# Sparse attention into a top-1 mixture of experts: v by 64-token tiles with neighbours copied in SBUF, loads farther ahead, x turned a tile ahead, lists used a pair later

## Chip, cores, metric

One core of one Trainium2 chip. The metric is the device time of one execution in microseconds (us), on the slowest (here the only) core. Before: 350.13 us, median of 3 runs (349.48 to 355.3).

## The reference

Block-sparse attention over 4 batches of 768 tokens with 8 heads of 64, then a mixture of 8 experts in which each token goes to one expert.

```python
# attention: block 32, window 16; 24 summary rows per head
k_sum = k.reshape(B, H, nb, block, D).max(axis=3)
v_sum = v.reshape(B, H, nb, block, D).mean(axis=3)
mask_l = np.abs(pos[:, None] - pos[None, :]) < window
# softmax over [q k^T masked by the window, q k_sum^T + log(block)], times [v, v_sum]
# experts, on x = attention output, 3072 x 512
logits = x @ w_gate + modality_bias[modality_id]
e_idx = np.argmax(logits, axis=1)
h = np.maximum(x[mask] @ w1[e], 0.0)                  # for each expert e
out[mask] = gate_w[mask, None] * (h @ w2[e])
```

## The kernel before

Attention works by pairs of heads: 16 pairs, 4 to a batch. A 64-token tile needs its own 64 keys and values, 16 neighbours on each side, and 24 summary rows. `features` turns the finished x of a pair, `route` picks experts after a batch, scatters the token rows to `xs` in DRAM (sorted by expert) and makes a list of tiles of 256 tokens of one expert; `expert_tile` computes one such tile. `pump()` puts one step of a tile between the steps of the next pairs, so that TensorE has two jobs to choose from. The last five tiles have no attention left beside them: the tail.

v goes from the load to a copy with a column of ones, to a scratch in DRAM, and back as overlapping windows:

```python
def values_in(n):
    vr = vrs[n % NV]
    nc.gpsimd.tensor_copy(vr[:, :, :, 0:D]..., vns.pop(n))
    nc.sync.dma_start(vscr[n % NV][16:S + 16]..., vr...)
def values_windows(n):
    nc.sync.dma_start(vws[n % NV][0:WK]...,
        bass.AP(a.tensor, a.offset, [[w, WK], [64 * w, NT], [1, w]]))
# ... (cut)
def expert_tile(i):
    xr = prep.pop(i)
    for c in range(NCD):
        for s2 in range(2):
            nc.tensor.transpose(px[:, c, s2, :], xr[:, s2, ts(c, 128)], ident)
    yield
    nc.vector.tensor_copy(xg, px...)
    # first layer ph (4 steps), Relu to hT, second layer pmo (2 steps), scaled rows to out (cut)
# ... (cut) the loop over pairs n = (b, cc)
    load(n + 3); scores(n, 1); values(n, 0); ...; values(n, 1); pump(); features(n)
    # list of batch b - 1 drained at cc == 0, its tiles from cc == 1, route(b) at cc == NP - 1
```

Names in the lines below: PE is TensorE, PEld its weight loads, DVE VectorE, ACT ScalarE, POOL GpSimd, SP SyncE with its DMA queue SPq. kn and qn are keys and queries as loaded, kb the keys with their neighbours, vw (later vb) the same for v, vs the summary rows of v and pv the matmuls that make them. pss are the scores, pT the masked weights, po the weighted values, xb the finished x, pt its turned (transposed) form. Of a tile, xr is x as loaded from `xs`, px its turned form and xg the copy of that, ph and pmo the matmuls of the two layers, ot the scaled rows. A line "A <- B" of the waits says that A stood idle until B was done.

The softmax here doesn't subtract the row's maximum and nothing guards it: scores larger than these inputs give would overflow.

## Time and profile before

| | before |
|---|---|
| span of the profiled execution | 358.2 us |
| first tile's turning px starts | 107.6 us |
| counts of the last batch known (pc) | 278.1 us |
| from first px to pc | 170.5 us |
| from pc to the end | 80.1 us |

These three stages are a first stage in which the DMA engines are nearly full, a middle in which tiles and attention share TensorE (PE), and an end. The busy totals (busy us, share of the span, instructions) say that no engine is near the bound over the whole span:

```profile
PE 198.4 (55%) x2359; PEld 135.1 (38%) x2359; DVE 137.7 (38%) x424; ACT 92.0 (26%) x169; POOL 107.9 (30%) x155
```

The profiled execution was some 8 us longer than the timed ones, which the prediction scales by 0.977; where in the span the excess lies isn't known.

In the middle alone, the windows view for PE (stretch, its length, PE busy us, granted clock, DMA share, GB/s):

```profile
107.60:278.10 170.50, 118.59 (x1379) 0.79 0.36 86
```

So 170.5 - 118.6 = 51.9 us of the middle are holes of PE.

### The profile page before, as it was taken

The page shows a single profiled execution, that of the slowest core. Times are in us where ns is not written, and L with a number is a line of the kernel's source. Part 1 is how long each engine was busy: PE and PEld are TensorE (multiplying, and loading weights), DVE is VectorE, ACT ScalarE, POOL GpSimd, SP SyncE. Part 2 cuts the span into 40 slices and gives each one's busy share as a digit, 9 for nine tenths or more (in the row PEclk, how much of TensorE's full clock was granted, in tenths as well). Part 3 has the DMA queues.
Part 4 walks back from the last instruction along what each step waited for, and adds up shares of the span by engine and source line. Part 5 has one row for each costly group of instructions (what it writes and reads, how often), then busy time and mean ns, then how long its engine had stood idle before and what let it go on. Part 6 is the DMA issues. An engine that isn't in the chain of part 4 may idle for free. (4 is left out here: it accounts for less than half of the span.)

```text
span 358.2 us, 6200 instructions
## 1 busy us (share of the span) xinstructions
PE 198.4 (55%) x2359; PEld 135.1 (38%) x2359; DVE 137.7 (38%) x424; ACT 92.0 (26%) x169; POOL 107.9 (30%) x155
## 2 busy tenths in 40 slices
PE   1140517264516957552395773969759003988860
PEld 1030416153404644341264542545536002566630
DVE  4230825458522336572124455523452700222210
ACT  1250316232501423151142412423302000222220
POOL 3981307006820050646003254021122510122220
PEclk9999999999999988855589885869897655899995
DMA  5999989943990253279431715050010273041110
GB/s 70 148 161 210 210 171 169 186 124 77 186 210 5 66 117 76 109 135 191 101 77 77 132 60 159 25 161 33 29 61 15 103 249 105 23 127 61 59 36 2
DMA packets 51606, 38.64 MB, mean 108 GB/s; under 512 B 29808, under 2 KB 46704, under 8 KB 51568
## 3 DMA queue, kind: packets, MB, share of 16 engines
q0 software_dynamic: 16880, 23.11, 31.9%
q1 hardware_dynamic: 34688, 15.06, 17.9%
q8 instruction: 20, 0.33, 0.4%
q14 instruction: 18, 0.15, 0.1%
HBM read 90.06 MB, written 15.58 MB: 295 GB/s over the span
## 5 line engine op out<-in xcount | busy, mean ns | idle before, releaser
L470 PE MATMUL ph<-xg,w1b 128*128 128x256 f16 x416 | 66.0, 323 | 34.5 <-DVE xg L464 31.7
L483 POOL DMA_INDIRECT out_dram<-ot,xr x26 | 25.9, 996 | 134.7 <-DVE ot L482 125.2
L470 PEld LDWEIGHTS <-w1b 128*128 128x128 f16 x416 | 45.0, 113 | 48.0 <-issue 36.4
L477 PE MATMUL pmo<-w2b,hT 128*128 128x512 f16 x208 | 50.8, 395 | 0.3 <-ACT hT L473 0.3
L473 ACT ACTIVATE hT<-ph 128x512 f16<-128x512 f32 x52 | 30.5, 599 | 74.7 <-PE ph L470 74.7
L257 ACT ACTIVATE pT<-pss 128x384 f16<-128x384 f32 x64 | 27.9, 486 | 52.1 <-PE pss L253 46.8
L358 POOL DMA_INDIRECT xs<-xb,posi x24 | 24.3, 1014 | 54.4 <-DVE tot L363 19.8
L258 DVE TENSOR_TENSOR pT<-pT,bmask 96x768 f16<-96x768 f16 x32 | 19.2, 600 | 45.6 <-ACT pT L257 45.2
L482 DVE TENSOR_SCALAR ot<-pmo,xr 128x512 f32<-128x512 f32 x26 | 19.3, 744 | 40.2 <-PE pmo L477 39.7
L272 PE MATMUL po<-vw,pT 120*64 120x65 f16 x384 | 15.3, 228 | 27.5 <-DVE pT L258 14.1
L461 PE MATMUL px<-ident,xr 128*128 128x128 f16 x104 | 9.2, 240 | 37.0 <-DMA xr<-xs 37.0
L233 ACT COPY qT<-pq 128x768 f16<-128x768 f16 x16 | 12.8, 802 | 63.0 <-PE pq L231 44.0
L477 PEld LDWEIGHTS <-hT 128*128 128x128 f16 x208 | 19.9, 100 | 22.9 <-issue 2.4
L217 ACT COPY kb<-pk 128x1152 f16<-128x1152 f16 x16 | 17.9, 1119 | 35.7 <-PE pk L215 28.7
L288 PE MATMUL pt<-ident,xb 128*128 128x128 f16 x96 | 12.9, 274 | 20.7 <-DVE xb L279 20.4
L272 PEld LDWEIGHTS <-pT 120*64 120x64 f16 x384 | 11.5, 137 | 33.7 <-issue 18.3
L461 PEld LDWEIGHTS <-xr 128*128 128x128 f16 x104 | 7.2, 108 | 38.8 <-DMA xr<-xs 37.1
L222 DVE TENSOR_TENSOR km<-kb 128x384 f16<-128x384 f16 x16 | 6.8, 426 | 38.4 <-ACT kb L217 38.4
L253 PE MATMUL pss<-qT,kb 64*128 64x64 f16 x384 | 14.9, 220 | 11.8 <-DVE kb L226 7.7
L92 POOL COPY vr<-vn 96x1024 f16<-96x1024 f16 x16 | 17.7, 1108 | 8.0 <-DMA vn<-in_v_dram 7.9
L279 DVE TENSOR_TENSOR xb<-po,rec 128x384 f16<-128x384 f32 x32 | 17.8, 557 | 1.3
L288 PEld LDWEIGHTS <-xb 128*128 128x128 f16 x96 | 7.8, 117 | 24.5 <-DVE xb L279 23.1
(123 smaller groups left out, 226.7 us busy)
## 6 DMA issues: line engine op xcount, KB each, us to landing
w1b<-in_moe_w_dram POOLq DMA_DIRECT2D x15, 1024.0 KB
w2b<-in_moe_w_dram POOLq DMA_DIRECT2D x15, 1024.0 KB
vw<-vscr SPq DMA_DIRECT2D x16, 292.5 KB
xr<-xs SPq DMA_DIRECT2D x13, 258.0 KB
vscr<-vr SPq DMA_DIRECT2D x16, 195.0 KB
kn<-in_k_dram POOLq DMA_DIRECT2D x16, 192.0 KB
qn<-in_q_dram POOLq DMA_DIRECT2D x16, 192.0 KB
vn<-in_v_dram POOLq DMA_DIRECT2D x16, 192.0 KB
```

Source lines behind the costliest of these rows:

```text
L217: nc.scalar.copy(kb[:, :, 0:WK].rearrange("p t (s c) -> p t s c", c=C8), bass.AP(pk.tensor, pk.offset, [pk.ap[0], [8, NT], [1, WK // C8], ...
L257: nc.scalar.activation(pT[:, h], pss[h], AF.Exp, scale=SCALE)
L258: nc.vector.tensor_tensor(pT[0:WK], pT[0:WK], bmask[0:WK, None, 6 * half:6 * half + 6, :].to_broadcast([WK, 2, 6, 64]), op=ALU.mult)
L272: nc.tensor.matmul(po[64 * (tl % 2):64 * (tl % 2) + 64, h, tl // 2, :], pT[0:KR, h, tl, :], vw[0:KR, 6 * half + tl, h, :])
L279: nc.vector.tensor_tensor(xo, po[:, :, :, 0:D], rec.unsqueeze(3).to_broadcast([128, 2, 3, D]), op=ALU.mult)
L288: nc.tensor.transpose(pt[:, c, :], xbs[b][:, c, ts(cc, 128)], ident)
L358: apart("xs", nc.gpsimd.indirect_dma_start(out=xs[:, :], out_offset=bass.IndirectOffsetOnAxis(ap=posi[:, c:c + 1], axis=0), in_=xb[:, c, : ...
L470: nc.tensor.matmul(ph[:, f, :], w1[:, c, ts(2 * f2 + f, 128)], xg[:, c, :], start=(c == 0), stop=(c == NCD - 1))
L473: nc.scalar.activation(hT[:, 2 * f2:2 * f2 + 2, :], ph, AF.Relu)
L477: nc.tensor.matmul(po, hT[:, f, ts(s2, 128)], w2[:, f, :], start=(f == 0), stop=(f == NF - 1))
L482: nc.vector.tensor_scalar_mul(ot, po, tl[:, 0:1].bitcast(FP32))
L483: apart("out", nc.gpsimd.indirect_dma_start(out=out[:, :], out_offset=bass.IndirectOffsetOnAxis(ap=tl[:, 1:2].bitcast(U32), axis=0), in_=o ...
```

## The change

The intent: take DRAM out of v's path, fill the holes around a tile's start, and begin the end's fills earlier. The diff, cut to its core:

```diff
 def load(n):                       # k, q as before
+    nc.gpsimd.dma_start(           # 1536 rows of 256 B, 64 tokens on 64 partitions
+        vbs[n % NV][0:64, :, :, 0:D]...,
+        v[b, 2 * cc:2 * cc + 2].rearrange("h (t p) d -> p (h t) d", p=64))
-def values_in(n): ...              # POOL copy, write of vscr
-def values_windows(n): ...         # read of the windows
+def halos(n):
+    nc.sync.dma_start(vb[64:80, :, 1:NT], vb[48:64, :, 0:NT - 1])
+    nc.sync.dma_start(vb[80:96, :, 0:NT - 1], vb[0:16, :, 1:NT])
 # keys: 64 own columns by ACT, two neighbour copies by POOL; pv: 12 matmuls from vb, was 8 from vr
-nc.sync.dma_start(mid, moe_modality_id.rearrange("(j p) -> p j", p=128))
+nc.sync.dma_start(midc, moe_modality_id.rearrange("(j p) -> j p", p=128))   # turned on PE
 def expert_tile(i):
+    if i not in xgs: turn(i); yield        # turn(i): px and its copy xg
     ... first layer ...
+    if i + 1 in prep: turn(i + 1)
     ... second layer ...
 # after pc in route():
+    if b == B - 1: fills(ci)               # was after the list
 # loop
-    load(n + 3)
+    load(n + 5)                            # six buffers
+    features(n - 1)                        # was features(n) after values(n, 1)
     # list drained at cc == 1 (was 0), its tiles from cc == 2 (was 1), route(b - 1) at cc == 0
```

Smaller pieces: in `route` the rows' positions are worked out ahead of the gate weights, the clearing of kb goes from POOL to DVE, and xg has three buffers instead of two.

## The prediction

> **What bounds the kernel now.** I read the page's slices first, then who waited for whom, then the timeline of the first 40 us, of one pair of heads in the middle, and of the end; last the windows and the DMA view by stretches. The slices (40 of 8.95 us each):
>
> ```profile
> PE   1140517264516957552395773969759003988860
> PEclk9999999999999988855589885869897655899995
> DMA  5999989943990253279431715050010273041110
> ```
>
> No engine is full over the span. There are four stages. Up to about 108 us the DMA engines are nearly full and PE is half idle. From 108 to 278 us PE is mostly busy with holes, and its granted clock is down in many slices. Then PE stands still for two slices, and five expert tiles follow. The same as windows (each engine's busy us, then granted clock, DMA share, GB/s):
>
> ```profile
> 36.00:78.00 42.00, 19.84 (x356) 15.45 (x357) 20.96 (x47) 13.42 (x25) 10.20 (x13) 1.00 0.98 176
> 190.00:250.00 60.00, 43.37 (x510) 27.61 (x509) 27.02 (x88) 18.68 (x36) 17.47 (x24) 0.80 0.35 90
> 278.00:300.00 22.00, 0.30 (x3) 0.04 (x2) 6.73 (x30) 0.00 (x0) 6.10 (x10) 0.56 0.48 165
> ```
>
> What PE, and DVE once, stood idle for (total us, times, longest):
>
> ```profile
> PE px L461 <- DMA xr<-xs: 37.0, 3, 22.2
> PE ph L470 <- DVE xg L464: 31.7, 12, 7.4
> PE pt L288 <- DVE xb L279: 20.4, 12, 7.3
> PE po L272 <- DVE pT L258: 14.1, 1, 14.1
> PE po L272 <- DMA vw<-vs: 8.1, 1, 8.1
> PE pss L253 <- DVE kb L226: 7.7, 1, 7.7
> PE po L272 <- DMA vw<-vscr: 5.3, 1, 5.3
> ```
>
> Each of these lines is one target of the change. The 14.1 us is the wait of DVE for the modality ids (midf waits 14.3 us, from 21.7 to 35.9 us): 3072 packets of 8 bytes, with every later DVE instruction held behind. The 31.7 us is the copy of the turned x in the expert tile. The 22.2 us is the gap before the tail:
>
> ```profile
> 278.37 0.17 DVE L379 CAST ci<-pc 128x8 int32<-128x8 f32 x1 [1.01 <-PE pc L370]
> 285.90 8.75 SPq L493 DMA_DIRECT2D xs<-fill  x8
> 297.32 20.30 SPq L449 DMA_DIRECT2D xr<-xs  x5
> 300.49 1.01 PE L461 MATMUL px<-ident,xr 128*128 128x128 f16 x8 [22.18 <-DMA xr<-xs]
> ```
>
> The counts are known at 278.5; the list takes DVE to 285.0; only then are the eight fills issued (8.75 us), land by about 297, x is loaded (3 us), and PE restarts at 300.5. A tile of the tail:
>
> ```profile
> 329.06 0.61 PE L461 MATMUL px<-ident,xr 128*128 128x128 f16 x8
> 330.66 3.65 PE L470 MATMUL ph<-xg,w1b 128*128 128x256 f16 x32 [0.99 <-DVE xg L464]
> 334.15 3.62 PE L477 MATMUL pmo<-w2b,hT 128*128 128x512 f16 x16
> ```
>
> The tail is bound by PE at 8.55 us a tile (329.06 to 337.60), of which 1.6 us lie from the turning's start to the first matmul of the next layer.
>
> **What the Trainium skill says.** (1) "TensorE: Matmul & The Clock Gate", Part 1: PE runs at half clock until about 3.4 us of sustained work, and falls back after an idle window of that length. The trace agrees: the first tile after the 22 us gap needs 6.39 us for its 32 ph matmuls, the next ones 3.65. So a hole costs more than its length. (2) "DMA: Bandwidth & Descriptors", Specifications and "Why small descriptors are slow": below 512 B a transfer leaves line rate, by a per-descriptor overhead. The trace agrees in direction: in 0 to 18 us software packets (nearly all the 2 KB rows of k, q, v) took 0.615 x 18 x 16 / 1700 = 104 ns each; in 72 to 90 us hardware packets (nearly all 260 B) took 0.365 x 18 x 16 / 4315 = 24 ns each, four times less time for eight times less source. (3) The same page, "Queues, rings and completion order": each engine takes turns between the queues it has work for, packet by packet. The trace shows that this doesn't make small transfers prompt: vw<-vs, issued at 40.8 us among weights and loads, held PE until 52.7.
>
> **The change, part by part.**
> *v path.* Removed per pair: the POOL copy vr (17.7/16 = 1.1 us), the write of vscr, and the read of 96 x 12 = 1152 rows of 260 B, a chain of three hops. Added: v itself comes in 64 x 24 = 1536 rows of 256 B in place of 192 of 2 KB; two halo copies of 32 long rows; the summary rows as 576 instead of 288. DMA time per pair before: 3 x 192 x 104 / 16 = 3.7 us for k, q, v, plus about 1540 x 24 / 16 = 2.3, in all 6.0. After: k and q 2.5; v at 25 to 60 ns a row is 2.4 to 5.8, I take 35 ns, 3.4; the rest 640 x 24 / 16 = 1.0; in all 6.9. So the engines get slightly more work, not less; what goes is latency: v's neighbours wait for nothing written to DRAM.
> *First stage.* DVE's 14.3 us wait goes (24 rows of 1 KB in place of 3072). kb no longer waits for POOL's memsets (6.9 us, they move to DVE, some 7 us of memsets there in the shadow of the first loads). Five pairs are loaded ahead, and the waits on vw (8.1 + 5.3) go. But DMA is 98% busy from 36 to 78 us, so these don't add up: the floor is the DMA work that must be done by the end of the seventh pair (n = 6), where the first tile may start: nine pairs' loads at 5.9 (53), three of the four weight loads at 1 MB / 176 GB/s = 6 us (18), the hardware queue (9), 4 us of start: 84. Before, that same pair ended at 122.6 with most of a tile in it; the fair comparison is the end of n = 5, 100.4, plus some 7 us for a bare pair and 7.2 us of wait for xr. I take 90, and 4 us for xr's load (below), against 115: 21 us less, and book 18, since queueing is not perfect.
> *Middle.* Holes for xg there are 27.0 us (7 times); px and the copy now run between the two layers of the tile before, so all but those of the first tile of a batch go: -22. Holes for xr were 6.8 and 8.0 us (the first is booked above). Now px stands directly behind the issue of xr's load in program order, so I leave 4 us each: -4. The pt waits (3.9 here, 16.5 before 108 us, where DMA is the floor) go, as features work one pair late: -3. pv has 12 matmuls instead of 8: 1.04 or 0.64 us becomes 1.5 or 0.96, +0.4 x 10 pairs = +4. Fewer holes keep the clock up (granted 0.80 in the window above): -5. A filled hole uncovers the next wait (ACT, DVE in order), so of the -30 I book -22.
> *End.* fills are issued right after the counts, beside the list: they start at about 279 instead of 285.9, -6.7. In the tail the 0.99 us wait and the turning's drain leave the chain: about 1.05 us for four of five tiles, -4.2 (the first has nothing before it). One half layer of the last overlapped tile slips into the gap, where PE is idle: 0. Together -10.
>
> Sum: 18 + 22 + 10 = 50 us on the profiled span, 358.2 to 308; times 350.1 / 358.2 for the timed runs: -49, **301 us**.
>
> **The rivals.**
> (a) *The v load becomes the bound.* 24 576 small software packets are added. At 100 ns a row instead of 35, v alone costs 9.6 us a pair and a pair 13 us of DMA: nine pairs are 117 us plus 18, the first stage gains nothing, and the result is 318 to 325. For: DMA is already full there; a row is short on both sides. Against: 24 ns for 260 B rows on the hardware queue, and 104 ns is what 2 KB cost at full rate.
> (b) *The old waits are replaced by a later one.* Lists are used one pair later, px of a batch's first tile has no lead over its load, and two pairs per batch have no tile work; the middle would gain some 8 us instead of 22: 315. For: xr took 7.6 us from issue to use at 100 us. Against: the long waits then were behind a burst of nine held-back loads, and these now run farther ahead.
> (c) *Everything adds up.* With PE warm throughout, the granted clock says up to a fifth of 43 us in 60 could go as well; the middle then gains 35 and the start 25: 281.
> A loss needs (a) far worse than 100 ns, or POOL blocked by its own descriptors at the start (five loads of 1920 rows are issued before its halo copies of the keys); the end's 10 us, nearly 3%, hardly depend on any of that.
>
> **Range and chances.** Centre 301 with (a) and (b) pulling to 320 and (c) to 282: 8 in 10 between 283 and 320. Faster by over 2% (under 343): 0.95; within: 0.04; slower: 0.01.
>
> **What would show it.** Right: midf no longer waits; no vw<-vscr or vw<-vs wait; the sixth copy of features (it now runs in the seventh pair) at about 87 to 97 us; the waits of ph on xg down from 31.7 to under 8; fills start within 2 us of the counts and the gap before the tail about 15 us; tail tiles 7.5 us apart; granted clock above 0.80 in the middle. Wrong: DMA at 9 past 110 us with PE waiting on kn or v (rival a); px waiting over 6 us three times (b); a new POOL wait ahead of kb's halo columns; or the middle still near 170 us though xg no longer waits, which would mean that PE's holes were only symptoms.

## More of the kernel before

What SyncE's (SP's) DMA queue waited for (total us, times, longest):

```profile
SPq L101 <- DMA vscr<-vr: 37.2, 8, 11.5
```

The load of v's windows stands in an in-order queue until its write to DRAM has landed, and what is behind it stands too.

## The result, and the profile after

The changed kernel took 293.97 us (median of 4 runs, 290.81 to 299.16; two of the four were slow), the kernel before 350.72 us beside it. The ratio of the fast runs is 0.8325, 95% interval 0.8248 to 0.8403. Ratios here are the mean time of one kernel's fast runs over that of the other's in the same rounds, so not quite the ratio of the medians. Executions over 1.5% slower than the fastest of the same kernel are left out of the means. The prediction (301, range 283 to 320, faster at 0.95) holds. Its parts are another matter.

The slices of the kernel after (40 of 7.23 us each: PE's busy tenths, its granted clock, DMA's busy share):

```profile
PE   1024776879311899945079998099698126999980
PEclk9999999999999999995559999579999675999996
DMA  8999999999999917695900302422302863041110
```

DMA is now full through the fourteenth slice (about 101 us), PE's dead slices before the tail are shorter, and the middle is denser. The middle as a window of PE:

```profile
94.90:223.00 128.10, 98.95 (x1324) 0.88 0.46 82
```

PE's holes fell from 51.9 to 128.1 - 99.0 = 29.1 us, and its busy time by 19.6 us, at a granted clock of 0.88 instead of 0.79. (One pair of the sixteen fewer lies in this window, so part of the 19.6 us is that pair's: the first px is one pair later in the program.) What PE waited for after:

```profile
PE px L468 <- DMA xr<-xs: 30.9, 4, 9.2
PE pv L240 <- DVE kp L138: 9.4, 1, 9.4
PE po L275 <- DVE pT L261: 9.4, 2, 6.7
PE pss L256 <- POOL kb L219: 8.6, 1, 8.6
PE pmo L493 <- DVE done L442: 6.9, 1, 6.9
PE po L275 <- DMA vb<-vs: 6.6, 4, 2.2
PE ph L484 <- DVE xg L470: 3.9, 4, 2.3
```

The waits on xg (31.7 us before), on xb (20.4) and on v's scratch are gone or small, and PE's wait for the turned modality ids is 4.2 us; xr, with four waits of 6.6 to 9.2 us, is the largest left. New are waits for POOL's neighbour copies, for pT and a list (done) behind small instructions on DVE, and, at the start, for DVE's setup (kp). What this last one costs, under the DMA work of the first stage, no run shows. The POOL wait in order of time (start us, us, instruction, idle before it and by what):

```profile
77.28 1.02 POOL L368 DMA_INDIRECT xs<-xb,posi  x1 [3.79 <-DMA w2b<-in_moe_w_dram]
83.05 0.98 POOL L368 DMA_INDIRECT xs<-xb,posi  x1 [2.18 <-DMA vb<-in_v_dram]
85.31 0.35 POOL L218 COPY kb<-kb 128x176 f16<-128x176 f16 x1
```

The keys were there at 73.0 us; the copy of 0.35 us stands behind six scatters in POOL's program order (72.4 to 85.3 us), and the trace puts the waits of two of them down to other DMAs. The prediction had named this wait as a sign of being wrong. The end:

```profile
223.20 0.17 DVE L375 CAST ci<-pc 128x8 int32<-128x8 f32 x1 [1.82 <-PE pc L373]
224.27 9.64 SPq L508 DMA_DIRECT2D xs<-fill  x8
...
237.19 2.84 SPq L453 DMA_DIRECT2D xr<-xs  x3
...
240.05 1.03 PE L468 MATMUL px<-ident,xr 128*128 128x128 f16 x8 [6.59 <-DMA xr<-xs]
...
255.15 0.61 PE L468 MATMUL px<-ident,xr 128*128 128x128 f16 x8
255.59 3.62 PE L493 MATMUL pmo<-w2b,hT 128*128 128x512 f16 x16
259.05 3.66 PE L484 MATMUL ph<-xg,w1b 128*128 128x256 f16 x32
262.54 0.61 PE L468 MATMUL px<-ident,xr 128*128 128x128 f16 x8
```

The fills start 1.1 us after the counts, px comes 17.1 us after pc (22.4 before), and a tail tile takes 7.39 us (255.15 to 262.54) instead of 8.55, its turning now between the layers of the tile before.

| | before | after |
|---|---|---|
| first px | 107.6 | 94.9 |
| first px to pc | 170.5 | 128.1 |
| pc to the end | 80.1 | 66.1 |
| span | 358.2 | 289.1 |

### The profile page after: what moved, and what is told of

It is laid out like the page before. It is cut to its first block, busy times and chain, and to the rows that moved or that the text cites. A ratio compares the mean times of both kernels' runs of the same rounds, so it can differ in the third digit from the quotient of the medians.

```text
span 289.1 us, 6359 instructions
## 1 busy us (share of the span) xinstructions
PE 188.4 (65%) x2424; PEld 133.8 (46%) x2424; DVE 140.8 (49%) x423; ACT 87.9 (30%) x169; POOL 101.5 (35%) x168
## 2 busy tenths in 40 slices
DMA packets 55723, 32.11 MB, mean 111 GB/s; under 512 B 37484, under 2 KB 52356, under 8 KB 55684
## 5 line engine op out<-in xcount | busy, mean ns | idle before, releaser
L499 POOL DMA_INDIRECT out_dram<-ot,xr x26 | 25.8, 994 | 95.9 <-DVE ot L498 89.3
L484 PE MATMUL ph<-xg,w1b 128*128 128x256 f16 x416 | 55.5, 289 | 3.9 <-DVE xg L470 3.9
L484 PEld LDWEIGHTS <-w1b 128*128 128x128 f16 x416 | 40.9, 103 | 13.4 <-issue 4.5
L261 DVE TENSOR_TENSOR pT<-pT,bmask 96x768 f16<-96x768 f16 x32 | 17.8, 556 | 38.9 <-ACT pT L260 38.8
L493 PEld LDWEIGHTS <-hT 128*128 128x128 f16 x208 | 19.8, 101 | 29.6 <-issue 10.4
L470 DVE COPY xg<-px 128x1024 f16<-128x1024 f16 x13 | 8.9, 687 | 43.0 <-PE px L468 43.0
L240 PE MATMUL pv<-vb,gsel 64*24 64x130 f16 x192 | 19.9, 274 | 9.4 <-DVE kp L138 9.4
L275 PE MATMUL po<-vb,pT 120*64 120x65 f16 x384 | 15.5, 223 | 16.0 <-DVE pT L261 9.4
L85 POOL DMA_DIRECT2D vb<-in_v_dram x16 | 15.7, 982 | 15.9 <-PE po L275 4.4
L240 PEld LDWEIGHTS <-gsel 64*24 64x24 f16 x192 | 16.0, 115 | 11.1 <-DVE kp L138 9.6
L275 PEld LDWEIGHTS <-pT 120*64 120x64 f16 x384 | 11.4, 132 | 20.9 <-DVE pT L261 11.3
L256 PE MATMUL pss<-qT,kb 64*128 64x64 f16 x384 | 13.9, 217 | 10.5 <-POOL kb L219 8.6
L256 PEld LDWEIGHTS <-kb 64*128 64x128 f16 x384 | 9.4, 109 | 17.4 <-POOL kb L219 8.9
```

The source lines that it names most:

```text
L240: nc.tensor.matmul(pv, gsel[0:64, ts(t, NB)], vb[0:64, :, t, :], start=(t == 0), stop=(t == NT - 1))
L256: nc.tensor.matmul(pss[h][:, tl, :], kb[rr, t, :], qT[rr, ts(t, 8), :].rearrange("p s c -> p (s c)"))
L261: nc.vector.tensor_tensor(pT[0:WK], pT[0:WK], bmask[0:WK, None, 6 * half:6 * half + 6, :].to_broadcast([WK, 2, 6, 64]), op=ALU.mult)
L275: nc.tensor.matmul(po[64 * (tl % 2):64 * (tl % 2) + 64, h, tl // 2, :], pT[0:KR, h, tl, :], vb[0:KR, h, 6 * half + tl, :])
L484: nc.tensor.matmul(ph[:, f, :], w1[:, c, ts(2 * f2 + f, 128)], xg[:, c, :], start=(c == 0), stop=(c == NCD - 1))
L493: nc.tensor.matmul(po, hT[:, f, ts(s2, 128)], w2[:, f, :], start=(f == 0), stop=(f == NF - 1))
```

## The experiments

Twelve kernels ran, all correct. Chips differ (the kernel before took 360.0 us on that of the first four runs, 354, 351 and 350 on the others), so each is compared by its ratio to the kernel before on its own chip. The kernel after was timed on one chip only: to set the others beside it takes its ratio to be the same on theirs, and its own interval alone is 2.7 us to either side. "us" derived from ratios are differences of ratios times 350. Traces give the place.

### Parts alone, on the kernel before

**The fills** right after the counts, and nothing else.

```diff
         nc.vector.tensor_copy(ci, pc)
+        if last:
+            fills(ci)
```

> The kernel before with one part of the change alone: the eight fills are issued right after the counts, before the list is made. Theory: the fills leave the chain ahead of the tail and nothing else moves; the 22.2 us hole of PE before the tail falls to 15 to 16.5 us and the time by 6 us (ratio to before 0.980 to 0.985). Rival: the fills were not the last link (the landing of the scatters or the list is); the hole stays above 20 us and the time falls by 2 us or less.

357.06 us, ratio 0.9827 [0.9734, 0.992]: 0.0173 x 350 = 6.1 us, by the interval 2.8 to 9.3. The profiled run was slow, so no lines of it are used. This fits the term of the prediction (-6.7).

**The modality ids** as 24 rows, turned on PE.

> The kernel before with one part alone: the modality ids come in as 24 rows of 1 KB, turned by one transposition on PE, in place of 3072 packets of 8 bytes, at the same place of the program. Theory (the first stage's floor is DMA work): DVE's 14.3 us wait goes, but the DMA engines were full during it, so only 3 to 8 us come back (ratio 0.978 to 0.991), and other waits on DMA (vw, kn, qn) grow. Rival (the waits of the first stage add up): 12 us or more come back (0.966 or less).

358.35 us, ratio 0.9935 [0.9882, 0.9987]: 2.3 us, under the 3 to 8 of the theory. The ids came sooner, but the wait did not go: DVE still stood 6.4 us for them, and PE, which now turns them, 17.7:

```profile
PE pm L202 <- DVE mh L200: 17.7, 1, 17.7
```

PE went on at 28.1 us instead of 36.6, and only 1.7 us of these 8.5 were left at the first px (105.9 instead of 107.6). That fits a first stage bound by DMA work; a start without the wait wasn't tried.

### Parts undone, on the kernel after

**Five pairs in flight** back to three, with the six buffers kept.

```diff
-        if n + 5 < np_:
-            load(n + 5)
+        if n + 3 < np_:
+            load(n + 3)
```

> The changed kernel with loads three pairs ahead instead of five (same six buffers). Theory: the depth hides the full DMA engines in the first stage; with three ahead the keys of a pair are waited for behind the weights, and the time grows by 5 to 12 us (298 to 305). Rival: the first stage is bound by the sum of DMA work, which the depth does not change, and loads far ahead only delay the scatters and the loads of x: the same within 3 us, or up to 4 us faster, with the 8.6 us wait of PE for POOL's halo copies of the keys gone.

301.39 us, ratio 0.8359 [0.8312, 0.8405] against 0.8325 [0.8248, 0.8403]: no difference shown, so depth alone isn't shown to give anything. The theory's wait did appear: PE stood for kn<-in_k_dram for 15.9 us in 6 times, against none among the waits of the kernel after, and the time didn't follow it. PE's wait for POOL's copies of kb went, as the rival had said.

**The early turning**: px and its copy again at the tile's own start.

```diff
-        if i not in xgs:
-            turn(i)
-            yield
+        yield from turn(i)
...
-        if i + 1 in prep:
-            turn(i + 1)
```

> The changed kernel with one part undone: x of every tile is turned at its own start again, its copy behind the yield as in the kernel before. Theory: the waits of ph for xg (3.9 us in the changed kernel) return to some 27 us, and the time grows by 20 to 28 us to 313 to 320 (ratio to before 0.89 to 0.91). Rival (the holes were a symptom, the work behind them would have waited anyway): 4 to 10 us more, 297 to 303, with the growth confined to the five tiles of the tail.

308.5 us, ratio 0.8568 [0.8514, 0.8623], so 8.5 us: the rival's range. PE's waits in this kernel:

```profile
PE ph L483 <- DVE xg L471: 25.8, 13, 9.0
PE px L468 <- DMA xr<-xs: 17.5, 3, 8.3
```

Undoing it brings back 21.9 us of waits on xg, but 13.4 us of the waits on xr go: where PE stands still for one thing, the next has arrived meanwhile. Most of the 8.5 us is in the tail, as the rival had said: with the stages of the kernel after scaled to this chip (by 360.04 / 350.72), the middle is an estimated 2.6 us longer (134.1 against 131.5) and the end 5.3 (73.2 against 67.9), with tail tiles of 8.55 us again.

**The order** of before: features in the pair's own turn, lists and tiles one pair earlier.

```diff
-        if n:
-            features(n - 1)
         values(n, 1)
-        if n and cc == 0:
-            router = route(b - 1)
+        pump()
+        features(n)
+        # list drained at cc == 0, tiles from cc == 1, route(b) at cc == NP - 1
```

> The kernel after with the order of before in one respect: features of a pair run in the same pair, the routing at the end of a batch's last pair, its list in the next pair, tiles from the pair after (one pair earlier than after). v's path, five pairs in flight and the early turning stay. Theory (the order is part of what made the middle shorter: pt waits of 20 us on the last values go): 4 to 12 us longer than after, ratio 0.845 to 0.87, with pt waiting on xb for 10 us or more and the first px about a pair earlier. Rival (the pair later is only delay, the tiles would start earlier and fill more of the holes): the same as after or up to 6 us shorter, ratio 0.815 to 0.835.

297.87 us, ratio 0.8428 [0.8342, 0.8514]: 3.6 us longer by the ratios, but the intervals overlap, so this alone isn't shown to cost anything. The theory's sign came all the same: pt waited for xb for 20.5 us in 8 times (20.4 before, none after). A wait that comes back is not yet a cost.

**Both** order and early turning undone.

> Both the order and the early turning undone at once. If the two gains stand in for one another (a hole filled by the one would have been filled by the other): under 20 us longer than after, ratio under 0.89. If each takes its own waits away and they add: turning 8 us (measured) plus order 4 to 12 us, so 12 to 20 us longer, ratio 0.868 to 0.89. If they need one another: over 25 us longer, ratio over 0.905; then most of the middle's gain is here, and v's path is nearly free.

324.64 us, ratio 0.9164 [0.9067, 0.9261]: 29.4 us, where the two alone make 8.5 + 3.6 = 12. I had attached the wrong words to the outcomes: a pair that costs little singly and much together is one in which each *stands in* for the other. It isn't that they fill the same holes: in the middle PE's holes are 134.1 - 98.4 = 35.7 us with the turning alone undone and, in the window below, 36.9 with both, the waits on xg 21.1 and 17.4. What differs is the pace of PE: the ph matmuls take 58.4 and 66.2 us. Why the new order keeps that pace without the early turning, no run shows. The prediction's number for this outcome (over 0.905) was right, what it concluded for v (nearly free) was not, as the runs on v's path below say.

How it costs is best seen between this run and the last one, which have the same order and differ in the turning alone. Both profiled runs were slow, so they are comparable with each other, not with the kernel after. PE in the middle, the order undone first (there with PE's weight loads, DVE, ACT and POOL after PE), then both undone:

```profile
92.90:229.20 136.30, 106.71 (x1411) 71.75 (x1412) 72.98 (x214) 47.51 (x95) 41.61 (x68) 0.87 0.47 82
```

```profile
95.30:250.50 155.20, 118.28 (x1411) 0.80 0.43 72
```

With the same 1411 matmuls PE is busy 11.6 us longer; the holes grow by only 155.2 - 118.3 - (136.3 - 106.7) = 7.3 us. The lost time is mostly in the matmuls themselves. A tile's first layer is four groups of eight matmuls ph. In the run with both undone, one tile begins like this:

```profile
141.66 0.50 PE L291 MATMUL pt<-ident,xb 128*128 128x128 f16 x3 [7.42 <-DVE xb L282]
...
152.45 1.03 PE L468 MATMUL px<-ident,xr 128*128 128x128 f16 x8 [3.07 <-DMA xr<-xs]
...
154.36 1.86 PE L483 MATMUL ph<-xg,w1b 128*128 128x256 f16 x8
156.15 0.38 PE L275 MATMUL po<-vb,pT 120*64 120x65 f16 x12
156.47 1.05 PE L483 MATMUL ph<-xg,w1b 128*128 128x256 f16 x8
```

The same eight matmuls take 1.86 us after the holes and 1.05 us some 2 us later; px, in the same way, takes 1.03 us here and 0.62 where PE has been busy. The granted clock goes with them: it is 0.53 up to the first group of ph and 1.00 after it.

```profile
152.40:156.40 4.00, 3.85 (x44) 0.53 1.36 162
156.40:162.00 5.60, 5.60 (x90) 1.00 0.87 42
```

In the profiled runs the 416 ph matmuls took 66.0 us before (323 ns each), 55.5 us after (289 ns), 55.6 with the order undone and 66.2 with both undone; 10.2 of the 10.5 us between before and after lie in the middle. With the turning alone undone they took 58.4 us, though PE waited for xg 25.8 us in 13 times: not every hole has this second price.

### v's path

**v through DRAM again**, everything else as after: rows of 2 KB, POOL's copy, scratch, windows.

```diff
-        nc.gpsimd.dma_start(vbs[n % NV][0:64, :, :, 0:D]..., v[...]...(p=64))
+        nc.gpsimd.dma_start(vn..., v[b, 2 * cc:2 * cc + 2].rearrange("h (p c) d -> p h (c d)", c=C8))
...
+    nc.gpsimd.tensor_copy(vr[:, :, :, 0:D]..., vns.pop(n))
+    nc.sync.dma_start(vscr[n % NK][16:S + 16]..., vr...)
...
-        nc.sync.dma_start(vb[64:80, :, 1:NT], vb[48:64, :, 0:NT - 1])   # and the other side
+        for p0, m, r0 in ((0, 64, 16), (64, 16, 0), (80, 16, 80)):
+            nc.sync.dma_start(vb[p0:p0 + m]..., window rows of vscr from r0)
```

> The kernel after with only v's path undone: v comes in 192 rows of 2 KB, POOL copies it, it goes to a scratch in DRAM and is read back as three sets of window rows; five pairs of loads in flight, the new order and the early turning stay. Theory (v's latency is hidden by five pairs of loads in flight, what counts is the sum of DMA work, which is about the same): within 4 us of the kernel after, ratio to the kernel before 0.825 to 0.845; first px at 93 to 99 us. Rival (the chain of POOL copy, write and read of the windows still holds po): 12 to 25 us longer than after, ratio 0.865 to 0.905, with waits of po on vb for 8 us or more in sum and first px after 103 us.

380.43 us, ratio 1.0802 [1.0722, 1.0882]: far outside both. The experiment was badly made, as its waits show:

```profile
PE pv L262 <- DMA vb<-vscr: 124.6, 14, 14.5
```

In the kernel after, pv (the sums for the summary rows) reads vb in the same half pair in which the halos are issued. With vb coming through DRAM, that put the whole chain before pv, fourteen times; in the kernel before, pv read the copy vr in SBUF. So it doesn't tell what before's path cost, but it does show what one early reader of a DRAM round trip costs: some 9 us each (124.6 / 14).

**The same with pv from vr**, as before had it.

> The run with v through DRAM was unfair to the kernel before: there pv, the first use of v, read the windows (124.6 us of waits of pv on vb<-vscr), while in the kernel before it reads the copy vr in the SBUF. This one is the same with pv from vr, so that the windows are first used two pairs later. Theory (v's path is nearly free once nothing reads the windows early, and what rows it saves in loads it pays in windows): 290 to 302 us on a chip where before takes 350, ratio 0.825 to 0.86, no wait on vscr above 3 us. Rival (the chain of three hops costs the kernel by itself, even two pairs ahead): ratio over 0.875, with po or pss waiting on vb, vr or POOL for 10 us or more in sum.

322.99 us, ratio 0.9192 [0.913, 0.9254]: 30.3 us longer than after, so the rival holds: v through DRAM, placed like this, costs about half of the whole gain. The first px comes at 115.8 us, 20.9 later than in the kernel after; pc at 251.3. The waits of PE and, in its own view, of SP's queue:

```profile
PE px L497 <- DMA xr<-xs: 38.8, 5, 10.8
PE po L304 <- DMA vb<-vs: 29.8, 6, 13.4
```

```profile
SPq L109 <- DMA vscr<-vr: 61.3, 15, 12.4
SPq L100 <- POOL vr L99: 29.7, 5, 8.7
```

No line names the windows as what PE waits for, which I had looked for. PE waits for the summary rows vb<-vs and for xr, which share SP's queue with window loads that wait for their scratch:

```profile
48.38 2.65 SPq L274 DMA_DIRECT2D vb<-vs  x2
51.13 4.09 SPq L100 DMA_DIRECT2D vscr<-vr  x1
67.10 1.80 SPq L109 DMA_DIRECT2D vb<-vscr  x3
```

```profile
63.67 0.38 PE L304 MATMUL po<-vb,pT 120*64 120x65 f16 x6 [13.41 <-DMA vb<-vs]
```

The write of 195 KB, issued by 55.2, let its reader go at 67.1: 12 us, in which SP issued nothing. The summary rows, issued by 51.0, ahead of that write, were used at 63.7: PE waited 13.4 us for them, against 2.2 at most in the kernel after. So here it wasn't the queue's order that held them; the DMA engines were over 90% busy in the slices from 48 to 64 us. What this doesn't separate: the path also moves more (38.65 MB against 32.11 in the whole run), so how much of the 21 us is the chain and how much the bytes stays open.

Nor is it quite the path of before. There a pair's windows are asked for later in the loop, after the summary rows; here right after the write, ahead of them. SP waited 61.3 us in 15 times for the scratch, 37.2 in 8 before. So 30.3 us may overstate what before's path cost; no run has it in its own place. One more estimate: with order and turning both undone the kernel is still 0.0836 x 350 = 29.3 us ahead of the kernel before; less the fills (6.1) and the ids (2.3), some 21 us are left for v's path together with the deeper loads and the smaller pieces. That makes v's path a third to a half of the gain.

**A second load of v's rows** to a buffer that nobody reads.

```diff
+        nc.gpsimd.dma_start(vx[n % 2][0:64, :, :, 0:D]..., v[...]...(p=64))
```

> The kernel after with v loaded a second time, in the same 1536 rows of 256 bytes per pair, to a buffer that nobody reads. It measures what such rows cost. Theory (25 ns a row on each of 16 engines, so 2.4 us a pair, and the first stage bound by the sum of DMA work): the first px moves from 94.9 by 9 to 10 pairs of 2.4 us, so 18 to 28 us later, to 113 to 123 us; the time grows by 15 to 28 us, ratio 0.875 to 0.915. Rival (a row costs 100 ns, as I had feared): 9.6 us a pair, over 60 us longer. Rival (the DMA engines are not what bounds the first stage): under 6 us longer.

338.5 us, ratio 0.9597 [0.9528, 0.9666]: 44.5 us longer, above the theory's range and below the rival of 100 ns. The slices of DMA (8.45 us each, full until about 194 us), and PE's longest wait:

```profile
DMA  9999999999999999999999903023220297223110
```

```profile
PE pss L260 <- POOL kb L223: 42.3, 5, 20.9
```

The first px moved from 94.9 to 136.6 us. From 9 pairs (needed by then) to 12 (issued by then) had gone in, and there are 96 such rows a pair on each engine: 41.7 us / (12 x 96) = 36 ns to 41.7 / (9 x 96) = 48 ns a row, an estimate of what the row costs when the engines are full. Part of it isn't the DMA engine but POOL: the copies of the keys' neighbours stood in its program order behind loads and six scatters, and PE waited up to 20.9 us for them. And the new buffer has two slots only, so a load into it may wait for an earlier one to land (POOL waited 9.1 us in 4 times for vx ahead of vx).

### Trying to beat the changed kernel

**The list behind pT on DVE** (one step of the router taken out of the middle of the pair), and the same **with the keys' neighbours copied by ACT**.

```diff
             summaries(n + 2)
-        if router and cc == 1:
-            step(router)
         pump()
...                                              # second kernel only
-        nc.gpsimd.tensor_copy(kb[:, 1:NT, 64:80], kb[:, 0:NT - 1, 48:64])
+        nc.scalar.copy(kb[:, 1:NT, 64:80], kb[:, 0:NT - 1, 48:64])
```

> The kernel after with one step of the router removed from the middle of the pair, so that the list's 22 small instructions come on DVE behind pT of the same half. Theory (the wait of po for pT behind the list, 9.4 us in two times in after, is on PE's path in the middle): that wait under 2 us, time 4 to 8 us shorter than after, ratio 0.81 to 0.822. Rival (PE then waits as long for xr, since the list ends as late): the waits of px on xr rise by what those of po fall, time within 2 us of after, ratio 0.827 to 0.838.

> The same, and the two copies of the keys' neighbours go from POOL to ACT, so that they don't stand behind scatters on POOL's queue. Theory (pss waited 8.6 us for them at 77 to 86 us, just ahead of the first px): first px 3 to 8 us earlier than 94.9 and the time 3 to 8 us below that of the kernel with the late list alone. Rival (the first stage is bound by the sum of DMA work, so the wait only moves): first px within 2 us of 94.9, time within 2 us of the late list's.

290.97 us (two fast runs, 289.31 and 288.14, too few for an interval) and 289.68 us, ratio 0.8207 [0.8135, 0.8279]. The interval overlaps that of the kernel after (0.8248 to 0.8403), so an advantage of some 4 us is possible and not shown. In the first kernel the targeted wait went and another grew:

```profile
PE po L275 <- DVE pT L261: 1.8, 1, 1.8
PE pss L256 <- POOL kb L219: 16.8, 2, 10.3
PE px L468 <- DMA xr<-xs: 27.3, 4, 9.0
```

In the second the wait on POOL is gone, yet the first px comes at 98.5 us (its profiled run was slow), against 97.7 in the first kernel and 94.9 in the kernel after, so not earlier. That fits the rival, for which this wait only covered DMA work. SP's queue in that kernel shows something else:

```profile
167.21 1.74 SPq L245 DMA_DIRECT2D vb<-vs  x2
187.13 0.40 SPq L453 DMA_DIRECT2D xr<-xs  x1
187.64 0.67 SPq L93 DMA_DIRECT2D vb<-vb  x1
```

For some 18 us nothing is issued: a load of x for an earlier list's tile waits for the scatters of a later batch, which come before it in program order though it needs none of their rows, and the neighbours' copies stand behind it.

**All x of a list loaded together** as soon as the list is there, ahead of those scatters (six buffers), on top of the two edits above.

```diff
-        if cc == 2 and new:
+        if cc == 1 and new:
+            hold[0] = new[0][2]          # tiles of this list start in the middle of cc == 2
+            for t in new:
+                rows(*t)                 # the xr load alone
             todo.extend(new)
```

> A version to beat the changed kernel: the late list, the keys' neighbours on ACT, and the loads of x for all tiles of a batch issued together at the end of the pair in which its list is made (six buffers), with the first tile's turning half a pair later. In the late-list kernel SP stood 16.6 us at a load of x for an earlier batch's fourth tile, waiting for scatters of a later batch that it doesn't need (they are ahead of it in program order), and the neighbours' copies, the summary rows and the next loads of x stood behind it. Theory: that wait and two of the three waits of px on xr in the middle (9.2 and 5.6 us) go: 8 to 16 us shorter than the late list's 290, so 274 to 283, ratio 0.785 to 0.805. Rival (the holes were filled by nothing else, but PE then waits for vb or pT instead): within 3 us of it, ratio 0.812 to 0.829.

290.09 us over 6 runs, ratio 0.8295 [0.8238, 0.8351]: the same as after; the rival holds. SP's wait on the scatters fell from 21.9 us in total (in the second kernel above) to 5.0, and PE's hole moved:

```profile
PE px L475 <- DMA xr<-xs: 45.7, 4, 19.8
```

The 19.8 us are the gap before the tail. The tiles run out earlier, so PE stands longer waiting for the last list (pc at 222.5, px at 242.5; in the kernel after 223.0 and 240.1). That suggests that what bounds these versions is when the last batch's counts are known, which depends on the attention pairs and not on tiles that start sooner; no run tested it by itself, and the gap from pc to px also grew, from 17.1 to 20.0 us. No version is shown to be faster than the changed kernel.

## Why the prediction was right, and where not

Its frame was an estimate of 115 us for the first px if the kernel before had placed it where the kernel after does. From that frame it said 94, the middle 141 (163 less 22) and the end 70; measured were 94.9, 128.1 and 66.1.

- **First stage: right in size.** The sixth copy of features ran at 87.9 us (predicted 87 to 97), px at 94.9 (94). The floor was DMA work, as said: the ids came 8 us sooner and gave 2.3, three pairs in flight weren't shown to do worse than five, and more rows moved px by 41.7 us. v's row was taken at 35 ns; the second load puts it at 36 to 48. Rival (a), 100 ns, is refuted. One reading is weaker than it looks: the share of a queue counts the time that its packets took, and in the kernel after the software queue's is 122% between 36 and 78 us. So 104 and 24 ns are times of packets that can overlap, not what one costs the engine, and that their sum came out at 94 is in part luck. "What goes is latency" fits v_dram_pv, whose first px is 20.9 us later, but the chain and the extra bytes were not told apart.
- **Middle: the right mechanisms, one term mis-sized.** Booked was -22 out of -30; against the same frame it was 128 - 163 = -35 (some of which may be the 8 us by which the profiled execution of before was long). The holes shrank by 22.8 us (51.9 to 29.1), near the 29 booked for xg, xr and pt before the discount. What was too small is the term "fewer holes keep the clock up (granted 0.80): -5": the 416 ph matmuls alone took 10.5 us less, and with the order fixed the turning changed PE's busy time by 11.6 us and the holes by 7.3. The prediction had said itself that a hole costs more than its length, from the Trainium skill and from a first tile of 6.39 against 3.65 us, and then booked little for it. The skill's page "TensorE: Matmul & The Clock Gate" has the very pattern, in its section "HAM oscillation — how this bites in real kernels": a loop whose every round waits longer than 3.4 us starts every round at half clock. The trace agrees in kind (1.86 against 1.05 us for eight matmuls, at a granted clock of 0.53 and then 1.00, after idle times such as 7.4 us), and I hadn't multiplied it by eight tiles. pv cost 5.2 us more over the whole run (14.7 to 19.9 us), about as booked (4).
- **The turning isn't worth 22 us by itself.** Credit went to one part where two share it: undone alone it costs 8.5 us (in the middle an estimated 2.6), together with the order 29. Its discount, "a filled hole uncovers the next wait", was right in kind: xr was that next wait.
- **xr: too hopeful.** Booked were 4 us for each load behind which px stands directly; measured were 7.2, 7.9 and 9.2. Rival (b)'s sign (px waiting over 6 us three times) appeared, and its time (315) didn't. Two more signs went against the prediction without its time failing: the POOL wait ahead of kb's neighbours (8.6 us), and waits on v's summary rows (6.6 us in all), which were to go.
- **End: -14 against -10.** The gap shrank by 5.3 (predicted 6.7; the fills took 9.64 us instead of 8.75), the tail's tiles by 4.9 (4.2). The remaining 3.7 us lie between the last scaling ot and the end of the span (11.85 to 8.1 us); no run explains them.
- **The whole.** Order with turning, and v's path, cost 29 and 30 us when undone; with the fills' 6 and the ids' 2 that is 67 for a gain of 0.1675 x 350 = 58.6: the parts overlap by some 8 us, or v_dram_pv overstates its own. The prediction was 7 us above the measured median (9 above the mean of the fast runs, 291.6), on the side of caution. On the profiled spans it said 50 us and 69.1 were measured, 8 of which may be the long execution of before. The clock's term is the largest of its mis-sized ones.

## What to carry to other kernels

Ask of a hole of PE two prices: its length, and the matmuls behind it (1.86 instead of 1.05 us for eight, at a granted clock of 0.53); the second is paid after some holes only, so look at the granted clock there. Judge a part by undoing it singly and together with whatever may stand in for it; here 8.5 and 3.6 became 29. And look for DRAM round trips in an in-order issuing queue: in v_dram_pv PE never waited for the windows by name, yet an estimated third to half of the gain was there.

## What the Trainium skill lacked or had wrong

- "TensorE: Matmul & The Clock Gate", Part 1, advises for models that "the ramp penalty is <1% of a typical kernel span". Here the half-clock time, which came back with the tiles, was larger: the 416 ph matmuls took 66.0 us in the kernel with holes at its tiles' starts and 55.5 us in the one without, 10.5 us or 3% of 358.2, from one kind of matmul alone. The page's own section on oscillation describes why.
- "DMA: Bandwidth & Descriptors", "Why small descriptors are slow", puts the overhead of a 256 B descriptor at 27% (11 cycles in place of 8). In this case a row of 256 B on the software queue, with the engines full, cost an estimated 36 to 48 ns per engine. No page was found with a trn2 figure for such rows under load.
- On no page did I find what it costs that GpSimd's compute stands behind the DMA issues and scatters of its own program order: in the changed kernel a copy of 0.35 us ran 12.3 us after its keys were there and PE waited 8.6 us for it; in the run with v loaded twice PE waited up to 20.9 us.
- The same DMA page, in "Anatomy of one DMA — SWDGE (gpsimd) path", has a fixed cost of about 2 us for setup and completion; that fit has no term for other work in the DMA engines, and no page was found that gives one (a remark on load concerns the latency of HBM alone). In the first stage of v_dram_pv, on the hardware queue and not the software queue of the fit, a write of 195 KB took about 12 us from issue until its reader was released (55.2 to 67.1 us).
